# A planner's computed instruction order replaced by a table of another order, in a fused retention and mixture-of-attention kernel

## The chip, the cores and the metric

The program runs on one core of a Trainium2 chip. The metric is the device time of one execution in microseconds (us), lower is better. TensorE is called PE in the rows (PEld are its weight loads), VectorE is DVE, ScalarE is ACT, GpSimd is POOL and SyncE, which issues all transfers here, is SP.

## The reference

Inputs are q, k and v of 4 batches, 8 heads, 768 steps and 64 features. A linear-attention recurrence with a decay per head makes y; its heads side by side are the input x (4 x 768 x 512) of four attention experts, of which each row uses two.

```python
for t in range(S):
    state = gamma[None, :, None, None] * state + np.einsum('bhd,bhe->bhde', k[:, :, t], v[:, :, t])
    y[:, :, t] = scale * np.einsum('bhd,bhde->bhe', q[:, :, t], state)
...
logits = x @ w_gate              # the two largest of 4: softmax weights
for e in range(E):
    q = x @ wq[e]
    k = x @ wk[e]
    v = x @ wv[e]
    scores = scale * (q @ k.transpose(0, 2, 1))
    scores = np.where(causal, -1000000000.0, scores)
    scores = scores - scores.max(-1, keepdims=True)
    a = np.exp(scores)
    a /= a.sum(-1, keepdims=True) + 1e-09
    ye = a @ v @ wo[e]
    ...                          # added to the output of the rows that chose e
```

## The kernel before

The work is cut along time. A *chunk* is 128 steps of a batch for all heads (24 in all). `chunk(g)` is three steps on TensorE: `h1(2g)`, `h2(g, g+1)` and `h1(2g+1)`. An `h1` takes the state's update of a half chunk (L486) and what the state gives to y (L490); `h2` takes the products inside the chunk (L545) and, for the next chunk, q times k (L551). All are 64x64 matmuls in fp32, 128 of them in a chunk as the profile counts them, each with a weight load. DVE evacuates the state into `sblk` (L500) and masks q times k into `am` (L559); GpSimd scales K and Q by decays ahead of it (`kdecay` L425, `qdecay` L440; DVE for chunk 0). ScalarE and DVE split y into a high and a low part, `xh` (L513) and `xl` (L516).

Three chunks are a *group* (8 in all), the unit of the attention. For a group TensorE makes four projections (`proj`, L601, 12 matmuls each) to q and k of a pair of experts; SP moves pieces of them between partitions (L618). Three value/gate products (`vgate`, L643) give v and the gate's logits. Max passes (`mpass`: L724, L737 and L738 on TensorE, L727 and L746 on DVE) find each row's maximum, which `mrow` moves through DRAM into an extra row of q. Then come scores (L850, L851) with the exponential on ScalarE (L857), the sums of its tiles (L872, L879; the first columns copied by ScalarE, L875), products with v (`av`, L896), the normalizer's sums (`norm_a`, L919) and output products (`wout`, L1010, evacuated at L1018).

None of these calls emits an instruction at once. A `Recorder` stores each as an operation with its engine, an assumed cost, the operations it depends on, and the tiles it needs. Tiles come from tags with few slots; all products but the state and `av` share tag `ps`, six PSUM banks. `schedule` then plays the operations through with the assumed costs and latencies, and each time takes the one with the least start time plus 0.01 of its rank; ranks come from the order of recording, of the last operations from the longest path (`by_path`), and are moved at random places by `shift` for 66 seeds. The result is a fixed order for each engine and a slot for each tile, and the program is emitted in it. Each engine works through its own instructions in that order and waits on semaphores where an operand or a slot is not ready. Before all this TensorE runs 12 warm-up matmuls (L1121) on a tile that GpSimd sets to zero, and SP issues the first loads: chunks' tiles `qkT_t` (L410) and `kv_t` (L414), constants (L360), and weight pieces (L379), which ScalarE, DVE and GpSimd split into high and low parts (L385, L386).

Of the kernel before, what the change touches and what calls it, by code (L numbers as in the profile page):

```python
# [3 lines left out]

# [10 lines left out]
AX = mybir.AxisListType  # L15

COL = 0.4545e-3
SWITCH = 0.17
LAT = dict(PE=dict(PE=0.0, DVE=0.2, ACT=0.2, POOL=0.26, SP=0.25),
           DVE=dict(PE=0.16, ACT=0.04, POOL=0.08, SP=0.1),  # L20
           ACT=dict(PE=0.16, DVE=0.04, POOL=0.08, SP=0.1),
           POOL=dict(PE=0.16, ACT=0.06, DVE=0.04, SP=0.1),
           SP=dict(PE=0.16, ACT=0.06, DVE=0.06, POOL=0.1, SP=0.1))
ALPHA = 0.01

COST = dict(chunk=2.2, proj=2.1, vg=1.44, m0=0.35, m1=0.6, g2=0.2, wout=1.4, norm=0.7, mrow=0.1)
MARGIN = 0.0
SWP = 2.0
LEAD_P = 0.0
PATH = 1.0  # L30
LEAD_A = 0.25

SHIFTS = (
# [3 lines left out]
)  # L37


def act_c(n):  # L40
# [11 lines left out]
class Buf:  # L52
    def __init__(self, tag):
        self.tag = tag
        self.slot = None
        self.left = 0
        self.made = None

    @property
# [2 lines left out]


class Tag:
    def __init__(self, tiles, name="", fifo=True):
        self.name = name
        self.fifo = fifo
        self.tiles = tiles
        self.free = [0.0] * len(tiles)
        self.owner = [None] * len(tiles)  # L70
        self.order = []
        self.next = 0


class Op:
    __slots__ = ("eng", "cost", "fn", "mode", "deps", "new", "bufs", "rank", "idx", "start", "end", "users",
                 "waiting", "nbytes", "at")


class Recorder:  # L80
# [6 lines left out]
    def op(self, eng, cost, fn, r=(), w=(), new=(), mode=None, nbytes=0):  # L87
        o = Op()
# [5 lines left out]
        deps = set()  # L94
# [16 lines left out]
            b.tag.order.append(b)  # L111
        o.bufs = {k[0] for k in (*r, *w) if isinstance(k[0], Buf)}
        for b in o.bufs:
            b.left += 1
# [7 lines left out]
    def by_path(self, first, scale):  # L122

        end = max(o.rank for o in self.ops)
        path = {}
        for o in reversed(self.ops):
            tail = path.get(o, 0.0) + o.cost + (1.7 if o.eng == "SP" else 0.0)
            for d in o.deps:
                t = tail + (0.0 if d.eng == o.eng and o.eng != "SP" else LAT[d.eng][o.eng])
                if t > path.get(d, 0.0):  # L130
                    path[d] = t
            if o.idx >= first:
                o.rank = end - scale * tail

    def shift(self, seeds):

        at = [o.rank for o in self.ops]
        span = max(at)
        for seed in seeds:
            rnd = random.Random(seed)  # L140
            w = rnd.choice((20, 40, 80, 400))
            a = rnd.uniform(-w / 2, span - w / 2)
            amp = rnd.choice((0.5, 1.5, 4, 10))
            engines = rnd.choice((("PE",), ("PE", "DVE", "ACT", "POOL", "SP"), ("DVE", "ACT", "POOL", "SP")))
            dens = rnd.choice((0.1, 0.3, 1))
            for o, t in zip(self.ops, at):
                if a <= t < a + w and o.eng in engines and rnd.random() < dens:
                    o.rank += rnd.gauss(0, amp)

    def schedule(self):  # L150
        users = {}
        for o in self.ops:
            o.users = []
        for o in self.ops:
            o.waiting = len(o.deps)
            for d in o.deps:
                d.users.append(o)
        ready = {}
        for o in self.ops:
            ready.setdefault(o.eng, [])  # L160
            if not o.waiting:
                ready[o.eng].append(o)
        T = {e: 0.0 for e in ready}
        mode = None
        bw = 0.0
        out = []
        lastfree = {}

        def est(o):
            t = T[o.eng]  # L170
            for d in o.deps:
                if d.eng == o.eng and o.eng != "SP":
                    e = d.end
                else:
                    e = d.end + LAT[d.eng][o.eng] + (MARGIN if o.eng == "PE" else 0.0)
                if e > t:
                    t = e
            need = {}
            for b in o.new:
                tag = b.tag  # L180
                k = need.get(tag, 0)
                if tag.fifo and tag.order[tag.next + k] is not b:
                    return None
                slots = sorted((tag.free[i], i) for i in range(len(tag.tiles)) if tag.owner[i] is None)
                if len(slots) <= k:
                    return None
                if slots[k][0] + 0.16 + MARGIN > t:
                    t = slots[k][0] + 0.16 + MARGIN
                need[tag] = k + 1
            return t  # L190

        n = len(self.ops)
        while len(out) < n:
            best = None
            for e, lst in ready.items():
                eb = None
                for o in lst:
                    s = est(o)
                    if s is None:
                        continue  # L200
                    sc = max(s, T[e]) + ALPHA * o.rank
                    if e == "PE" and o.mode != mode:
                        sc += SWP * SWITCH
                    if eb is None or sc < eb[0]:
                        eb = (sc, s, o)
                if eb and (best is None or eb[1] < best[1]):
                    best = eb
            assert best is not None, [(o.idx, o.eng) for l in ready.values() for o in l][:20]
            _, s, o = best
            for b in o.new:  # L210
                tag = b.tag
                _, i = min((tag.free[i], i) for i in range(len(tag.tiles)) if tag.owner[i] is None)
                tag.owner[i] = b
                b.slot = i
                tag.next += 1
            o.start = s
            if o.eng == "PE":
                if o.mode != mode:
                    s += SWITCH
                    mode = o.mode  # L220
                o.end = T["PE"] = s + o.cost
            elif o.eng == "SP":
                T["SP"] = s + 0.4
                bw = max(bw, s + 0.4) + o.nbytes / 300e3
                o.end = bw + 1.7
            else:
                o.end = T[o.eng] = s + o.cost
            for b in o.bufs:
                b.left -= 1
                b.tag.free[b.slot] = max(b.tag.free[b.slot], o.end)  # L230
                if not b.left:
                    b.tag.owner[b.slot] = None
            ready[o.eng].remove(o)
            out.append(o)
            for u in o.users:
                u.waiting -= 1
                if not u.waiting:
                    ready[u.eng].append(u)
        self.span = max(o.end for o in out)
        self.busy = {e: sum(o.cost for o in out if o.eng == e) for e in T}  # L240
        self.out = out
        return out

    def replay(self):

        T = {}
        free = {}
        mode = None
        bw = 0.0
        for o in self.out:  # L250
            s = T.get(o.eng, 0.0)
            for d in o.deps:
                s = max(s, d.at if d.eng == o.eng and o.eng != "SP" else d.at + LAT[d.eng][o.eng])
            for b in o.new:
                s = max(s, free.get((b.tag, b.slot), 0.0) + 0.16)
            if o.eng == "PE":
                if o.mode != mode:
                    s += SWITCH
                    mode = o.mode
                o.at = T["PE"] = s + o.cost  # L260
            elif o.eng == "SP":
                T["SP"] = s + 0.4
                bw = max(bw, s + 0.4) + o.nbytes / 300e3
                o.at = bw + 1.7
            else:
                o.at = T[o.eng] = s + o.cost
            for b in o.bufs:
                k = (b.tag, b.slot)
                free[k] = max(free.get(k, 0.0), o.at)
        return max(o.at for o in self.out)  # L270


@with_exitstack
def tile_retention_moe_attention(
# [881 lines left out]
    for s in range(1, NJ):  # L1156
# [3 lines left out]
        merge(ls, (0.0, LEAD_P, LEAD_A))  # L1160
    merge([tail[:]])
    tail[:] = []
    first = len(R.ops)
    merge([stream_p(NJ - 1)])
    merge([stream_a(NJ - 2)])
    merge([stream_a(NJ - 1)])

    if PATH:
        R.by_path(first, PATH)
    R.shift(SHIFTS)  # L1170
    order = R.schedule()
    with tc.manual_schedule():
        for o in order:
            o.fn()


_SHAPES = [((4, 768, 512), "float32")]

# [76 lines left out]
```

## Time and profile before

| | |
|---|---|
| time, median of 3 runs | 330.72 us (329.74 to 331.65) |
| span of the profiled execution, first to last instruction | 326.7 us |
| between that span and the median of the runs | 4.0 us |
| busy: TensorE, its weight loads | 314.3 us (96%), 272.9 us (84%) |
| busy: DVE, ScalarE, GpSimd | 174.7 us (53%), 132.6 us (41%), 170.3 us (52%) |
| chain that ended last, by engine | PE 88%, DMA 7% |
| transfers | 50.82 MB, mean 156 GB/s |

The profile tells of one execution. A busy share is a mean over stages with different limits, so what matters is where the busiest engine stands still, and what ended each such stop. "issue" means that an instruction began late though nothing that the profile shows was waited for. All times are counted from the start of the span.

### The profile page before, as it was taken

To read this page: it belongs to the slowest core of one execution; us is meant where nothing else is said; L and a number is where in the kernel's file an instruction comes from. 1 tells how busy PE (TensorE), PEld (TensorE's weight loads), DVE (VectorE), ACT (ScalarE), POOL (GpSimd) and SP (SyncE) were. 2 spreads that over 40 slices of the span, in tenths; PEclk is the share of its full clock that TensorE was granted. 3 is DMA by queue.
4 is the path that set the end of the run, shared out by engine and by line. 5 is a ranking of instruction groups with operands and counts; after the bars stand their busy time and mean duration, and the time that the engine had idled before them with its cause. 6 is when DMAs were issued, how large, how long until landed. Compare 5 with 4: busy or idle time off the path is not lost.

```text
span 326.7 us, 11233 instructions
## 1 busy us (share of the span) xinstructions
PE 314.3 (96%) x4738; PEld 272.9 (84%) x4738; DVE 174.7 (53%) x478; ACT 132.6 (41%) x322; POOL 170.3 (52%) x189
## 2 busy tenths in 40 slices
PE   7779999999999999999999999999999999999995
PEld 3669989889978799879979788897979789878674
DVE  2574467666443555767242574937452243896733
ACT  1452222533535333524527224432534235428542
POOL 5776251561874976314785854542394361913700
PEclk9999999999999999999999999999999999999999
DMA  7996993355468353535563675352412422413022
GB/s 261 357 403 226 283 324 117 112 142 179 106 188 266 136 181 102 161 124 181 145 160 135 197 237 144 142 164 86 114 45 99 98 49 74 125 69 91 1 99 96
DMA packets 22071, 50.82 MB, mean 156 GB/s; under 512 B 3618, under 2 KB 8310, under 8 KB 22020
## 3 DMA queue, kind: packets, MB, share of 16 engines
q1 hardware_dynamic: 22020, 50.10, 49.0%
q8 instruction: 37, 0.61, 0.8%
q14 instruction: 14, 0.11, 0.1%
HBM read 30.71 MB, written 6.79 MB: 115 GB/s over the span
## 4 chain that ended last, share of the span: by engine, by line
PE 88%; DMA 7%; issue 1%; SPq 1%; DVE 1%; ACT 1%; ACTq 0%
PE ps L601 20%; PE ps L1010 11%; PE ps_o L896 11%; PE ps L643 9%; PE ps L850 7%; PE ps L851 6%; PE ps_st L486 5%; PE ps L551 4%; PE ps L738 4%; DMA kv_t<-in_kv_dram 3%; PE ps L545 2%; DMA qkT_t<-in_qkT_dram 2%; PE ps L490 2%; PE ps L919 2%; PE ps L724 2%; PE ps_st L896 1%
## 5 line engine op out<-in xcount | busy, mean ns | idle before, releaser
L746 DVE CUSTOM_DVE_ANT_0 scr<-ps,cmask_t 128x128 bf16<-128x128 f32 (+3 forms) x64 | 29.7, 487 | 46.6 <-PE ps L738 46.1
L857 ACT ACTIVATE pt<-ps 128x384 f32<-128x384 f32 (+2 forms) x112 | 49.4, 491 | 12.1 <-PE ps L851 9.7
L440 POOL TENSOR_TENSOR qd<-qkT_t,qdec_t 128x512 f32<-128x512 f32 (+1 forms) x23 | 28.3, 1232 | 41.4 <-PE ps L490 26.2
L601 PE MATMUL ps<-xh,qk_hi 128*128 128x384 f32 x128 | 44.1, 345 | 0.0
L850 PE MATMUL ps<-q,k 128*128 128x384 f32 (+2 forms) x144 | 43.4, 316 | 0.0
L601 PE MATMUL ps<-xh,qk_lo 128*128 128x384 f32 x128 | 43.1, 337 | 0.0
L601 PE MATMUL ps<-xl,qk_hi 128*128 128x384 f32 x128 | 43.1, 336 | 0.0
L851 PE MATMUL ps<-q,k 65*128 65x384 f32 (+2 forms) x144 | 42.1, 312 | 0.0
L879 POOL TENSOR_TENSOR ac<-ac,pt 128x256 f32<-128x256 f32 (+2 forms) x32 | 39.9, 1247 | 3.1 <-ACT pt L857 1.2
L863 POOL TENSOR_SCALAR_AFFINE_SELECT pt<-pt 128x256 f32<-128x256 f32 x48 | 20.1, 426 | 38.9 <-ACT pt L857 38.2
L896 PE MATMUL ps_o<-pt,vt 128*64 128x384 f32 (+2 forms) x252 | 36.2, 422 | 0.0
L606 ACT ACTIVATE k<-ps 128x384 fp32r<-128x384 f32 x32 | 15.7, 491 | 50.0 <-PE ps L601 50.0
L425 POOL TENSOR_TENSOR kv_t<-kv_t,kdec_t 128x512 f32<-128x512 f32 (+1 forms) x23 | 22.2, 968 | 23.0 <-DMA kv_t<-in_kv_dram 23.0
L486 PE MATMUL ps_st<-kv_t 64*64 64x64 f32 x704 | 30.2, 222 | 1.7 <-POOL kv_t L425 0.7
L490 PE MATMUL ps<-qd,sblk 64*64 64x64 f32 x704 | 29.8, 221 | 0.8 <-issue 0.8
L872 POOL TENSOR_TENSOR ac<-pt,pt 128x512 f32<-128x512 f32 (+1 forms) x14 | 21.3, 1523 | 17.5 <-ACT pt L857 17.1
L486 PEld LDWEIGHTS ps_st<-kv_t 64*64 64x64 f32 x704 | 24.9, 134 | 6.2 <-issue 4.0
L896 PEld LDWEIGHTS ps_o<-pt,vt 128*64 128x64 f32 x252 | 16.4, 136 | 16.0 <-issue 11.9
L513 ACT ACTIVATE xh<-ps 128x512 fp32r<-128x512 f32 x24 | 14.3, 598 | 37.4 <-PE ps L490 35.6
L643 PE MATMUL ps<-vg_hi,xh 128*128 128x260 f32 x96 | 28.0, 291 | 1.5 <-ACT xh L513 1.5
L850 PEld LDWEIGHTS ps<-q,k 128*128 128x128 f32 x144 | 27.3, 190 | 2.4 <-issue 2.0
L500 DVE TENSOR_TENSOR sblk<-ps_st,sdec_t 128x256 f32<-128x256 f32 x44 | 18.5, 420 | 19.8 <-PE ps_st L486 18.4
(115 smaller groups left out, 777.6 us busy)
## 6 DMA issues: line engine op xcount, KB each, us to landing
qkT_t<-in_qkT_dram SPq DMA_DIRECT2D x24, 512.0 KB
kv_t<-in_kv_dram SPq DMA_DIRECT2D x24, 512.0 KB
out_dram<-ot SPq DMA_DIRECT2D x24, 256.0 KB
q<-k SPq DMA_DIRECT2D x28, 192.0 KB
k<-k SPq DMA_DIRECT2D x14, 192.0 KB
k<-q SPq DMA_DIRECT2D x14, 192.0 KB
fe<-fd SPq DMA_DIRECT2D x28, 96.0 KB
pt<-in_wqk_dram SPq DMA_DIRECT2D x4, 256.0 KB
```

The lines of the kernel that those rows point to most:

```text
L440: e.tensor_tensor(halves(qd.t), halves(qb.t[:, 0]), K["qdec"][:, :, None, :].to_broadcast([128, HP, n, SC]), op=OP.mult)
L486: nc.tensor.matmul(ST[b].t[rows(rt), s * D:(s + 1) * D], kvs(m, 0, s)[rows(rt)], kvs(m, 1, s)[rows(rt)], start=c == 0 and s == 0, stop=Fal ...
L490: nc.tensor.matmul(yo(m, rt, s), SB[m % 2][rows(rt), s], LD[g, 2].t[rows(rt), s, m % 2 * SC:(m % 2 + 1) * SC], start=m % 2 == 0 and s == 0 ...
L601: nc.tensor.matmul(pb.t[:, :HS], ww[:, kt, wsl], xx[:, kt], start=n == 0, stop=n == 11)
L643: nc.tensor.matmul(pb.t[:, :NV + E], xx[:, kt, sl], ww[:, kt], start=n == 0, stop=n == 11)
L746: lambda: nc.vector.tensor_tensor_reduce(scr.t[:, :n1], pb.t[:, :n1], K["cmask"][:, HS + C - n1:], 1.0, mx0.t[:, e, i:i + 1] if prior else ...
L850: nc.tensor.matmul(o, k1.t[:, e, ko:ko + C], q1.t[:, e, q0:], start=True, stop=False)
L851: nc.tensor.matmul(o, k2.t[:65, e, ko:ko + C], q2.t[:65, e, q0:], start=False, stop=True)
L857: lambda es=es, sb=sb, n=n: nc.scalar.activation(pt.t[:, es[0]:es[0] + n, q0:], sb.t[:, :n * w].rearrange("p (e t) -> p e t", e=n), AF.Exp ...
L879: op(eng, cost, lambda: en.tensor_tensor(ac.t[:, :, q0:], ac.t[:, :, q0:], pt.t[:, :, q0:], op=OP.add), r=[(pt, 0), (pt, 1), (ac, "b")], w ...
L896: nc.tensor.matmul(ob.t[e * 64:e * 64 + 64, q0:HS], vt.t[:, ko // C, ee * 64:ee * 64 + 64], pt.t[:, e, q0:], start=kb == 0, stop=kb == las ...
L1010: nc.tensor.matmul(wb.t, oo[:, sl], ww[:, p], start=n == 0 and p == 0, stop=n == 2 and p == NP - 1)
```

## The change

The operations, their dependencies and what each emits stay as they are. `schedule`, `by_path`, `shift` and `replay` go, with their constants. In their place stand two tables: `ORDER`, 1,555 numbers of operations in the order in which they are emitted, and `SLOTS`, which gives the slot of each new tile by tag. `arrange` looks both up. The table is not what the planner computed: on TensorE 213 of 510 operations keep their place in the engine's order, and on SP 59 of 224.

```diff
-    def schedule(self):
...
+    def arrange(self, order, slots):
+
+        turns = {name: iter(row) for name, row in slots.items()}
+        out = [self.ops[i] for i in order]
+        for o in out:
             for b in o.new:
...
+                b.slot = int(next(turns[b.tag.name]))
         return out
...
-    if PATH:
-        R.by_path(first, PATH)
-    R.shift(SHIFTS)
-    order = R.schedule()
     with tc.manual_schedule():
-        for o in order:
+        for o in R.arrange(ORDER, SLOTS):
             o.fn()
+
+ORDER = (
+    3, 1, 2, 5, 6, 4, 7, 12, 8, 13, 9, 10, 14, 19, 20, 21, 99, 0, 23, 100, 101, 102, 103, 26, 1313, 24, 25, 22, 28,
...
+SLOTS = {
+    "ac": "010101010101010101",
```

The first place is SP's queue, from its eighth issue on; the seven before it are the same transfers with the first K/V tile put first. In the names, `ot`, `ac` and `pt` are tiles that hold weight pieces at the start (value/gate, then q/k). Before:

```order
L410 DMA qkT_t_64<-in_qkT_dram 128x1024
L379 DMA ot_127<-in_wvg_dram 128x260
L379 DMA ot_128<-in_wvg_dram 128x260
L379 DMA ac_116<-in_wvg_dram 128x260
L379 DMA ac_117<-in_wvg_dram 128x260
L414 DMA kv_t_67<-in_kv_dram 128x1024
L410 DMA qkT_t_65<-in_qkT_dram 128x1024
L414 DMA kv_t_68<-in_kv_dram 128x1024
L379 DMA pt_110<-in_wqk_dram 128x512
```

And now:

```order
L245 DMA qkT_t_64<-in_qkT_dram 128x1024
L249 DMA kv_t_67<-in_kv_dram 128x1024
L214 DMA ot_127<-in_wvg_dram 128x260
L245 DMA qkT_t_65<-in_qkT_dram 128x1024
L214 DMA ot_128<-in_wvg_dram 128x260
L214 DMA ac_116<-in_wvg_dram 128x260
L249 DMA kv_t_68<-in_kv_dram 128x1024
L245 DMA qkT_t_63<-in_qkT_dram 128x1024
L214 DMA ac_117<-in_wvg_dram 128x260
L214 DMA pt_110<-in_wqk_dram 128x512
```

The K/V tile of chunk 1 and the q/k tiles of chunks 2 and 3 (`qkT_t_65`, and `qkT_t_63` for the second time) now stand among the value/gate pieces or ahead of them; line numbers are lower by 165 in the changed kernel. On TensorE the first value/gate product moves from before chunk 1 to behind chunk 2's first half, and the second to behind chunk 2.

The second place is TensorE at the border of chunks 17 and 18, the end of a batch (near 186 us before). The first row below ends chunk 17's products; then come chunk 17's last half, chunk 18's first half and its `h2`. Before:

```order
L545 MATMUL ps_141<-am_72,kv_t_68 64x64
L490 MATMUL ps_141<-qd_70,sblk_156 64x64 x8
L486 MATMUL ps_st_147<-kv_t_66 64x64 x8
L551 MATMUL ps_144<-qkT_t_64 64x64
L545 MATMUL ps_145<-am_71,kv_t_66 64x64
```

And now:

```order
L325 MATMUL ps_143<-qd_70,sblk_156 64x64 x8
L321 MATMUL ps_st_147<-kv_t_66 64x64 x8
L845 MATMUL ps_144<-wo_hi,oh_121 128x512
L845 MATMUL ps_144<-wo_lo,oh_121 128x512
L845 MATMUL ps_144<-wo_hi,ol_123 128x512
L845 MATMUL ps_144<-wo_hi,oh_122 128x512
L845 MATMUL ps_144<-wo_lo,oh_122 128x512
L845 MATMUL ps_144<-wo_hi,ol_124 128x512
L573 MATMUL ps_141<-k_4_87,q_0_77 128x256
L754 MATMUL ps_145<-ac_116,sel 32x128 x2
L754 MATMUL ps_145<-ac_117,sel 32x128 x2
```

Between chunk 18's first half and its `h2` there now stand an output product, a max pass and the normalizer's 12 sums (24 matmuls in the profile; the first rows of them are shown).

The third place is TensorE at the last projections of group 5 (near 203 us before), where a max pass reads keys of a projection before. The first rows end a projection. Before:

```order
L601 MATMUL ps_144<-xh_74,qk_hi 128x384
L601 MATMUL ps_144<-xl_76,qk_hi 128x384
L601 MATMUL ps_144<-xh_74,qk_lo 128x384
L737 MATMUL ps_145<-k_1_84,q_1_78 128x384
L738 MATMUL ps_145<-k_2_85,q_1_78 128x128
L737 MATMUL ps_140<-k_1_84,q_1_78 128x384
L738 MATMUL ps_140<-k_2_85,q_1_78 128x128
```

And now:

```order
L436 MATMUL ps_145<-xh_74,qk_lo 128x384
L436 MATMUL ps_141<-xh_74,qk_hi 128x384
L436 MATMUL ps_141<-xl_76,qk_hi 128x384
L436 MATMUL ps_141<-xh_74,qk_lo 128x384
...
L436 MATMUL ps_141<-xh_74,qk_lo 128x384
L572 MATMUL ps_142<-k_3_86,q_1_78 128x384
L573 MATMUL ps_142<-k_2_85,q_1_78 128x128
```

The group's fourth projection (into `ps_141`) now stands between the third and the first max pass, which is followed by a value/gate product.

## Rows read from the trace of the kernel before

**Rows 1.** The page: busy time, share, instructions; and an instruction queue.
```profile
PE 314.3 (96%) x4738; PEld 272.9 (84%) x4738; DVE 174.7 (53%) x478; ACT 132.6 (41%) x322; POOL 170.3 (52%) x189
...
q8 instruction: 37, 0.61, 0.8%
```

**Rows 2.** Windows: length, busy us by engine (instructions), granted clock, DMA share, GB/s.
```profile
0.00:25.00 25.00, 18.72 (x451) 14.10 (x452) 12.92 (x28) 9.21 (x21) 17.29 (x26) 1.00 0.95 341
25.00:100.00 75.00, 74.25 (x1281) 67.87 (x1284) 41.06 (x119) 26.16 (x66) 36.74 (x39) 1.00 0.62 187
```

**Rows 3.** Timeline of TensorE: start, length, what, and the idle time before it.
```profile
20.21 0.27 PE L545 MATMUL ps<-am,kv_t 64*64 64x64 f32 x1 [0.95 <-issue]
45.50 0.21 PE L490 MATMUL ps<-qd,sblk 64*64 64x64 f32 x1 [0.75 <-issue]
188.57 0.27 PE L486 MATMUL ps_st<-kv_t 64*64 64x64 f32 x1 [0.47 <-issue]
203.86 0.33 PE L738 MATMUL ps<-k,q 128*128 128x128 f32 x1 [0.76 <-DMA k<-q]
225.86 0.30 PE L919 MATMUL ps<-ac,sel 128*32 128x128 f32 x2 [0.38 <-issue]
```

**Rows 4.** Waits of the weight loads after 25 us: total, times, longest.
```profile
PEld ps_o L896 <- issue: 11.9, 63, 0.4
PEld ps_st L486 <- issue: 4.0, 15, 0.6
PEld ps L490 <- issue: 0.9, 1, 0.9
```

**Rows 5.** Windows, from one stall's end to the next one's.
```profile
20.21:45.50 25.29, 23.58 (x636) 22.11 (x637) 13.88 (x29) 6.96 (x17) 11.71 (x12) 1.00 0.87 286
45.50:188.56 143.06, 142.60 (x2291) 127.16 (x2290) 76.08 (x217) 58.72 (x142) 84.99 (x89) 1.00 0.53 161
188.56:225.85 37.29, 36.15 (x510) 32.45 (x511) 22.78 (x58) 14.26 (x37) 17.06 (x20) 1.00 0.49 149
```

**Rows 6.** Windows: two code blocks of 64x64 work, and one chunk.
```profile
42.04:45.50 3.46, 2.71 (x142) 2.44 (x135) 2.40 (x5) 0.60 (x1) 1.73 (x2) 1.00 0.89 260
107.33:110.43 3.10, 3.10 (x130) 2.32 (x128) 0.79 (x2) 0.05 (x1) 3.02 (x4) 1.00 0.00 0
28.74:30.76 2.02, 2.02 (x129) 1.95 (x128) 1.24 (x3) 0.49 (x1) 0.00 (x0) 1.00 0.13 33
```

**Rows 7.** Timeline of TensorE in the first 25 us.
```profile
10.97 0.39 PE L643 MATMUL ps<-vg_hi,xh 128*128 128x260 f32 x1 [0.74 <-ACT xh L513]
16.19 0.24 PE L486 MATMUL ps_st<-kv_t 64*64 64x64 f32 x1 [0.67 <-POOL kv_t L425]
24.36 0.28 PE L643 MATMUL ps<-vg_hi,xl 128*128 128x260 f32 x1
24.48 0.34 PE L601 MATMUL ps<-xh,qk_hi 128*128 128x384 f32 x1
24.65 0.34 PE L601 MATMUL ps<-xl,qk_hi 128*128 128x384 f32 x1
```

**Rows 8.** Timeline of DVE: a weight split.
```profile
9.41 0.85 DVE L386 TENSOR_TENSOR vg_lo<-ot,vg_hi 128x260 fp32r<-128x260 f32 x1 [0.68 <-ACT vg_hi L385]
```

**Rows 9.** Waits of TensorE in the first 25 us: total, times, longest.
```profile
PE ps L643 <- ACT xh L513: 1.5, 2, 0.7
PE ps L551 <- DMA qkT_t<-in_qkT_dram: 0.7, 2, 0.4
PE ps_st L486 <- DVE kv_t L425: 0.5, 1, 0.5
```

**Rows 10.** Lines: a max pass on DVE; count, busy us, mean ns, idle before.
```profile
L727 DVE TENSOR_REDUCE mx<-ps 128x1 f32<-128x384 f32 x32 | 16.9, 552 | 8.2 <-PE ps L724 8.0
```

**Rows 11.** Timeline of ScalarE: the copy before which an output product was evacuated.
```profile
134.53 0.41 ACT L875 ACTIVATE ac<-pt 128x256 f32<-128x256 f32 x1
```

More of the change, by code (lines that the diff above doesn't have):

```diff
@@ L17 @@
 COL = 0.4545e-3
[L18 to L24, printed above, removed]
 COST = dict(chunk=2.2, proj=2.1, vg=1.44, m0=0.35, m1=0.6, g2=0.2, wout=1.4, norm=0.7, mrow=0.1)
-MARGIN = 0.0
-SWP = 2.0
 LEAD_P = 0.0
-PATH = 1.0
 LEAD_A = 0.25
-SHIFTS = (
[3 rows of a table removed]
-)
 def act_c(n):
@@ L55, in __init__ @@
         self.slot = None
-        self.left = 0
         self.made = None
@@ L64, with __init__ @@
 class Tag:
-    def __init__(self, tiles, name="", fifo=True):
+    def __init__(self, tiles, name, fifo=True):
         self.name = name
@@ L68, in __init__ @@
         self.tiles = tiles
-        self.free = [0.0] * len(tiles)
-        self.owner = [None] * len(tiles)
         self.order = []
-        self.next = 0
 class Op:
-    __slots__ = ("eng", "cost", "fn", "mode", "deps", "new", "bufs", "rank", "idx", "start", "end", "users",
-                 "waiting", "nbytes", "at")
+    __slots__ = ("eng", "cost", "fn", "mode", "deps", "new", "bufs", "rank", "idx", "nbytes")
 class Recorder:
@@ L113, in op @@
         for b in o.bufs:
-            b.left += 1
             if b in o.new:
@@ L120, in op @@
         return o
[L122 to L148, printed above, removed]
@@ L150, in schedule @@
-    def schedule(self):
[L151 to L178, printed above, removed]
-            for b in o.new:
[L180 to L241, printed above, removed]
-        return out
@@ L244, in replay @@
[L244 to L270, printed above, removed]
+    def arrange(self, order, slots):
+        turns = {name: iter(row) for name, row in slots.items()}
+        out = [self.ops[i] for i in order]
+        for o in out:
+            for b in o.new:
+                b.slot = int(next(turns[b.tag.name]))
+        return out
@@ L1162, in tile_retention_moe_attention @@
     tail[:] = []
-    first = len(R.ops)
+    R.first = len(R.ops)
     merge([stream_p(NJ - 1)])
@@ L1166, in tile_retention_moe_attention @@
     merge([stream_a(NJ - 1)])
-    if PATH:
-        R.by_path(first, PATH)
-    R.shift(SHIFTS)
-    order = R.schedule()
     with tc.manual_schedule():
-        for o in order:
+        for o in R.arrange(ORDER, SLOTS):
             o.fn()
+ORDER = (
[74 rows of a table added]
+)
+SLOTS = {
+    "ac": "010101010101010101",
+    "am": "010101010101010101010101",
+    "f": "0000000",
+    "fd": "0101010",
+    "fe": "0000000",
+    "ge": "0000",
+    "gg": "0000",
+    "gs": "0000",
+    "k1": "0123402134201324",
+    "k2": "0123402134201324",
+    "kv_t": "012012012012012012012012",
+    "lg": "0101",
+    "md": "01010101010101",
+    "mt": "01010101010101",
+    "mx": "0101010101010101",
+    "mx0": "01010101",
+    "mz": "00",
+    "oh": "0101010101010101",
+    "ol": "0101010101010101",
+    "on": "0120120120120120",
+    "ot": "01210210102102102102102102",
+    "ps": (
+        "0123450123450214352104315204135024150315251340512340152401523150423510431502413052341035412035410235"
+        "4120530241503245132405324102540314034013520143051234051350423502315024531204135021432045301254021543"
+        "0251243025413024530125032513041520301254310243512043125043210451320415203452104320135401253142503142"
+        "5312403512105421305421305241254352041530421350421350214351203451205312035410324510324124530125402531"
+        "405231405231502"
+    ),
+    "ps_o": "00000000000000",
+    "ps_st": "000000",
+    "pt": "012345021354021354021354021354021354021354021354021354021350214350503214503214",
+    "q1": "0120120120120120",
+    "q2": "0120120120120120",
+    "qd": "010101010101010101010101",
+    "qkT_t": "012012012012012012012012",
+    "rw": "010101",
+    "scr": "011010011010101010101010100110101001101000101010100110101010101010101010101001011001101001010010",
+    "vt": "01201201",
+    "wn": "0101",
+    "wt": "0101",
+    "xh": "01010101",
+    "xl": "01010101",
+}
 _SHAPES = [((4, 768, 512), "float32")]
```

1 line of the change is left out of this document (removed), and 76 rows, old and new, of tables (ORDER, SHIFTS).

## The prediction

> **What bounds the kernel now.** I read the page first. TensorE is busy 96% of the span and no other engine more than 53% [rows 1]. So an order of instructions can only win back time in which TensorE stands still, or lose more. Next the span by stretches: of the first 25 us TensorE works 18.72, of the following 75 it works 74.25, at a granted clock of 1.00, the upper level of 2.4 GHz, in both [rows 2]. So two things are open to an order: the first 25 us with 6.3 us idle, and the few stalls behind them.
>
> In the timeline after 25 us four stalls of TensorE are longer than 0.3 us. One, of 0.76 at 203.86, ends with a DMA; three, of 0.75, 0.47 and 0.38, end on "issue", on nothing that the profile shows [rows 3]. They lie in the middle of runs of small matmuls whose operands do not change there. A fourth of that kind, of 0.95, is at 20.21 [rows 3]. The weight loads, which run ahead of the matmuls, stand somewhat longer: 0.9 for the first, 0.6 for the second [rows 4].
>
> What do the "issue" stalls share? Between one and the next TensorE ran 636+637, 2291+2290 and 510+511 matmuls and loads [rows 5]: 1273, 4581 and 1021, which is 5, 18 and 4 times about 255. The page has 4738+4738 of them and 37 transfers on the instruction queue q8 [rows 1], so 256 instructions to a transfer. The stalls stand at borders of blocks of code, and I take them for waits for the next block. Whether a border stalls would then depend on how fast the block before it is used up: the block from 42.04 on, nothing but 64x64 matmuls, took 3.46 us with its stall, so 2.7 by TensorE's own work, and one of 3.10 passed without any [rows 6].
>
> The Trainium skill ("Runtime: NRT & Kernel Launch", section "Instruction fetch mechanics") also has code come in blocks of 256 instructions, but calls the cost of a crossing "mostly hidden". The trace agrees on the size; of 37 crossings it shows four that are not hidden. By that sentence alone the second term below would be nought.
>
> **The change part by part.** The same instructions run; their places and tile slots are others. The sum is made against the profiled execution: its span is 326.7, and the runs' median of 330.72 has 4.0 us around it, left as they are.
>
> *The first 25 us.* Before, SP issues all four value/gate weight pieces ahead of the second K/V tile, shown in the first excerpt above. TensorE does the first value/gate product at 10.97 after a wait of 0.74, reaches chunk 2's first half at 16.19 after 0.67 more for GpSimd's decay of K, and the first projection at 24.48 [rows 7]. Now chunks 1 and 2 come first, and their tiles are loaded first. Chunk 2's first half hardly moves all the same: the state goes through DVE, where the new order puts two weight splits (0.85 was one [rows 8]) and an xl ahead of the evacuation of chunk 1's state, while the pieces to split land later. I take 16.0. Behind it stand three value/gate products instead of two, but one of them now covers the wait for xh and xl of chunk 2 (up to 0.7), and the wait for a q/k tile (up to 0.4) goes, since that tile is loaded earlier [rows 9]. The work from there on is a chunk, 2.0 us as from 28.74 to 30.76 [rows 6], and three products of 12 matmuls at 0.12 from start to start [rows 7], 1.45 each: 6.4. The block stall of 0.95 stays, as the border falls into the same chunk: 7.3. The projection starts at about 23.3 to 23.5: **-1.0 us**. Bounds: -2.2 (no block stall either) and +0.5 (DVE holds chunk 1 up for longer).
>
> *Three block stalls.* In the first dense block the new order sets two max passes between the chunks, and a max pass and a whole projection ahead of the second chunk's last half; in the second an output product, a max pass and the normalizer's sums (the second excerpt above); in the third the sums are followed by an output product and max passes in place of chunk work before them. Each adds over 1.5 us to blocks of 2.4 to 2.7, which takes them past the 3.10 that passed [rows 6]. No other block behind the first 25 us becomes noticeably denser than it was where it passed. So -(0.75+0.47+0.38) = -1.6 by the matmuls [rows 3], and -1.9 with the loads' 0.9 and 0.6 for the first two [rows 4]: I take **-1.9**; nought if other borders stall instead.
>
> *The DMA wait at 203.86* (0.76 [rows 3]) is for a copy of keys between partitions. The new order puts a second projection ahead of the max pass that waits (third excerpt): 12 matmuls of 0.17 from start to start [rows 7], 2.0 us, which covers it. **-0.8**, or nought if the copy is issued later by as much.
>
> *New waits.* (a) At about 60 to 64 us the last projection of its group is moved behind a row of max passes, so six of these follow each other with four score products between. DVE needs about 0.55 for each [rows 10], TensorE 0.2 to 0.4, and six PSUM banks lie between them. Price 0 to 1.6; I take 0.5. (b) At about 135 us ScalarE's evacuation of an output product went ahead of an exponential and a copy (0.41 [rows 11]); now it stands behind both, and its bank is held longer by the copy and about as much for the exponential. Price 0 to 0.8; I take 0.3. (c) Max passes or scores nearer to what they need at about 204, 271 and 279 us: 0 to 1.6; I take 0.3. Together **+1.1** (0 to 4.0).
>
> *Tile shapes.* TensorE changes between 64x64, 64-column, 32-column and full tiles 81 times instead of 75. The nearest row is what the loads of the av products wait for "issue", 11.9 us in 63 cases [rows 4], so 0.19 for one, or 0 where hidden. Six more are 0 to 1.1; I take **+0.4**.
>
> Costed at nothing: the memset that the warm-up matmuls wait for comes two memsets later, but the first chunk waits 0.5 us for DVE's decay of K anyhow [rows 9]. Without that cover it is 0.7. The end of the program is the same output product in both.
>
> Sum: -1.0 - 1.9 - 0.8 + 1.1 + 0.4 = -2.2: a span of 324.5, and 330.7 - 2.2 = **328.5 us**.
>
> **The rivals.**
> 1. *The stalls go and nothing comes for them.* The first 25 us give 2.0, the stalls 2.7, six shapes cost 0.2: 330.7 - 4.5 = 326.2. For it: no engine that TensorE waits for is over 53% busy [rows 1]. Against it: the bunches of (a) and (b) can be read in the order.
> 2. *The "issue" stalls stay.* If a border stalls for what the instruction queue does just then and not for density, three of them are left or others stall: -1.0 - 0.8 + 1.1 + 0.4 = -0.3, so 330.4. For it: 3.10 passed, hardly more than the blocks that stalled, and dense ones are left. Against it: all four fell into the densest stretches. (The skill's sentence, with crossings hidden, would give this time too.)
> 3. *Slower: the banks fill.* The place is the bunches of (a) to (c). If DVE and ScalarE fall behind by more than six banks hold, TensorE waits as long as they lag: the prices at their upper ends are 4.0, shapes 1.1, the first 25 us 0, so 5.1 - 1.9 - 0.8 = +2.4: 333.1. It decides once the new waits and shapes together pass 4 us. For it: DVE's 0.55 against TensorE's 0.2 for a max pass. Against it: from 25 to 100 us DVE works only 41 of 75 us [rows 2].
>
> That the change doesn't do what it says is excluded: the excerpts show other orders on SP and TensorE.
>
> **How the numbers follow.** Forecast 0.52, rival 1 0.18, rival 2 0.18, rival 3 0.12. A measurement of this kernel can tell about 0.5%, 1.65 us, from no change. The forecast lies 2.2 below with about 1.3 to either side, so two thirds to three quarters of its 0.52 are faster and the rest the same; with all of rival 1 and a little of rival 2 that makes 0.60 faster, 0.29 same and 0.11 slower. The likeliest case alone has 327.2 to 329.8. The range takes in rivals 1 and 2 and ends half way to rival 3: 325.6 to 331.8.
>
> **What would show it.** In the changed kernel the first projection starts before 24 us; after 25 us no "issue" stall of 0.4 us or more is left in the 64x64 runs; the DMA wait near 200 us is gone; and the longest new waits are those of max passes or score products near 60 us. I am wrong if "issue" stalls of the old length stand at other borders of 256, if the projection starts at 24.5 or later, or if TensorE's waits after 25 us pass 4 us in all.

## The result and the profile after

The changed kernel takes 327.93 us (median of 12 runs, 326.41 to 329.93), the kernel before, on the same chip, 330.92 us (12 runs, 329.02 to 332.65). The ratio is 0.9915, with a 95% interval of 0.9886 to 0.9944: faster, by 3.0 us or 0.9%, a small change but clear of the noise. The forecast was 328.5. Times here and below are medians of all runs, while ratios and intervals are of the fast runs alone, those within 1.5% of the quickest of their kernel. The total came out nearly as forecast; several of its terms did not.

The page of the changed kernel, as in [rows 1]:

```profile
PE 315.4 (97%) x4738; PEld 274.7 (84%) x4738; DVE 172.3 (53%) x478; ACT 130.1 (40%) x322; POOL 169.7 (52%) x189
...
q8 instruction: 37, 0.61, 0.7%
```

The same instructions run, and TensorE is as busy. Next the windows as in [rows 2], with two stretches of the first 25 us by themselves (length, busy us of each engine, granted clock, DMA share, GB/s):

```profile
0.00:25.00 25.00, 18.50 (x436) 14.41 (x437) 11.18 (x26) 6.67 (x12) 15.70 (x24) 0.86 0.95 347
25.00:100.00 75.00, 74.58 (x1272) 68.19 (x1270) 42.68 (x124) 27.36 (x71) 38.10 (x40) 1.00 0.60 175
15.00:20.00 5.00, 3.94 (x87) 3.52 (x79) 4.17 (x8) 3.16 (x6) 2.47 (x3) 0.63 1.01 373
20.00:25.00 5.00, 5.00 (x113) 4.70 (x113) 1.15 (x3) 0.60 (x1) 2.79 (x2) 0.69 1.04 387
```

The start did not get better. TensorE works 0.2 us less in it than before, and from 15 to 25 us the granted clock is 0.63 and 0.69: for part of the time it stood at the lower of its two levels, 1.2 GHz. The waits of TensorE in the first 25 us say what came first (as in [rows 9]; total, times, longest):

```profile
PE ps L380 <- issue: 2.3, 1, 2.3
PE ps L956 <- POOL wu L917: 2.3, 1, 2.3
PE ps_st L321 <- POOL kv_t L260: 0.7, 1, 0.7
PE ps_st L321 <- issue: 0.6, 1, 0.6
PE ps_st L321 <- DVE sblk L335: 0.5, 1, 0.5
PE ps L380 <- DVE am L394: 0.2, 1, 0.2
```

The waits for xh (1.5) and for a q/k tile (0.7) are gone. In their place stands one "issue" stall of 2.3 us in a chunk's second half (line 380, which was line 545 before: all lines of the kernel stand 165 lower now). The timeline has it at 14.54, and the first projection (line 436) at 26.45, where [rows 7] had 24.48:

```profile
14.54 0.21 PE L380 MATMUL ps<-am,kv_t 64*64 64x64 f32 x1 [2.26 <-issue]
...
15.74 0.27 PE L321 MATMUL ps_st<-kv_t 64*64 64x64 f32 x1 [0.51 <-DVE sblk L335]
...
17.04 0.34 PE L321 MATMUL ps_st<-kv_t 64*64 64x64 f32 x1 [0.56 <-issue]
...
26.45 0.34 PE L436 MATMUL ps<-xh,qk_hi 128*128 128x384 f32 x1
```

Behind the first 25 us nearly all waits of TensorE are gone; the waits view of 25 to 330 us has this one row, where [rows 3] had four stalls:

```profile
PE ps L436 <- issue: 0.4, 1, 0.4
```

It is at 49.38, in the projection that the new order put into the first dense block. The max pass whose second matmul waited at 203.86 for the copy of keys (line 738, now 573) now runs at 206.14 and 206.33 without a wait, right behind the projection set ahead of it:

```profile
205.96 0.34 PE L436 MATMUL ps<-xh,qk_lo 128*128 128x384 f32 x1
206.14 0.35 PE L572 MATMUL ps<-k,q 128*128 128x384 f32 x1
206.33 0.22 PE L573 MATMUL ps<-k,q 128*128 128x128 f32 x1
```

From the first projection to TensorE's last matmul the changed kernel took 295.9 us, and the profiled execution of before 298.7. So against that execution the start lost 2.0 us and the rest won 2.8.

### The profile page after: what moved, and what is told of

Read it like the earlier page. It is cut to its first block, busy times and chain, and to the rows that moved or that the text cites. A ratio compares the mean times of both kernels' runs of the same rounds, so it can differ in the third digit from the quotient of the medians.

```text
span 325.9 us, 11205 instructions
## 1 busy us (share of the span) xinstructions
PE 315.4 (97%) x4738; PEld 274.7 (84%) x4738; DVE 172.3 (53%) x478; ACT 130.1 (40%) x322; POOL 169.7 (52%) x189
## 3 DMA queue, kind: packets, MB, share of 16 engines
HBM read 30.71 MB, written 6.79 MB: 115 GB/s over the span
## 4 chain that ended last, share of the span: by engine, by line
PE 94%; DMA 3%; DVE 1%; issue 1%; ACT 1%; SPq 0%; ACTq 0%; DVEq 0%
PE ps L436 21%; PE ps L478 11%; PE ps L845 11%; PE ps_o L731 10%; PE ps L685 7%; PE ps L686 7%; PE ps_st L321 6%; PE ps L386 5%; PE ps L573 4%; PE ps L559 2%; PE ps L325 2%; PE ps L380 2%; PE ps L754 2%; DMA ot<-in_wvg_dram 2%; PE ps_st L731 1%; DMA am_t<-in_amask_dram 1%
## 5 line engine op out<-in xcount | busy, mean ns | idle before, releaser
L698 POOL TENSOR_SCALAR_AFFINE_SELECT pt<-pt 128x256 f32<-128x256 f32 x48 | 20.9, 445 | 50.1 <-ACT pt L692 39.8
L685 PE MATMUL ps<-q,k 128*128 128x384 f32 (+2 forms) x144 | 43.9, 318 | 0.0
L686 PE MATMUL ps<-q,k 65*128 65x384 f32 (+2 forms) x144 | 42.2, 313 | 0.0
L731 PE MATMUL ps_o<-pt,vt 128*64 128x384 f32 (+2 forms) x252 | 35.5, 421 | 0.0
L380 PE MATMUL ps<-am,kv_t 64*64 64x64 f32 x768 | 27.8, 223 | 2.5 <-issue 2.3
L478 PE MATMUL ps<-vg_hi,xh 128*128 128x260 f32 x96 | 28.8, 300 | 0.0
```

Of the source, the lines that this page charges most:

```text
L380: nc.tensor.matmul(yo(2 * g + u, rt, s), kvs(u + 2 * g, 1, s)[rows(rt)], amg.t[rows(rt), u, s], start=g % NC == 0 and u == 0 and s == 0, s ...
L478: nc.tensor.matmul(pb.t[:, :NV + E], xx[:, kt, sl], ww[:, kt], start=n == 0, stop=n == 11)
L685: nc.tensor.matmul(o, k1.t[:, e, ko:ko + C], q1.t[:, e, q0:], start=True, stop=False)
L686: nc.tensor.matmul(o, k2.t[:65, e, ko:ko + C], q2.t[:65, e, q0:], start=False, stop=True)
L731: nc.tensor.matmul(ob.t[e * 64:e * 64 + 64, q0:HS], vt.t[:, ko // C, ee * 64:ee * 64 + 64], pt.t[:, e, q0:], start=kb == 0, stop=kb == las ...
```

## The experiments

Theory (T): the gain is in the order behind the start, by the borders of code blocks. Rivals: the new start makes the gain; the places of the tiles make it; fewer waits make it, whatever the borders. Each set of runs had the kernel before beside it, with medians of 331.27 us (e1 to e4), 332.77 (e5 to e8) and 330.93 (e9 to e12); ratios are to it.

### The kernel before, once more, and with its borders moved

The first (e3_before_again) is the kernel before, without an edit:

> The kernel before, unchanged, to see a second profile and the clock of each run. Theory: the same three issue stalls at the same instructions, the DMA wait, first projection at 24.5 us and no fall of the clock in most runs. Rival: other runs of it lose time in the first 25 us too, as the changed kernel does, and the profile shown was a lucky one (a span of 327.5 or more).

It took 331.05 us (10 runs). This execution, close to its median, loses more in the same places than the one shown first:

```profile
21.87 0.27 PE L545 MATMUL ps<-am,kv_t 64*64 64x64 f32 x1 [1.85 <-issue]
...
26.13 0.34 PE L601 MATMUL ps<-xh,qk_hi 128*128 128x384 f32 x1
...
47.71 0.21 PE L490 MATMUL ps<-qd,sblk 64*64 64x64 f32 x1 [1.30 <-issue]
```

The stalls of 0.95 and 0.75 [rows 3] are 1.85 and 1.30 here, the first projection starts at 26.13, not 24.48, and the rest takes 299.8 us. Its span is 329.5 and its time 331.22: 1.7 us lie around a span, in this and in every other execution profiled whose time is known, but for e6 (2.1). So the execution of [rows 1 to 11], with a span of 326.7, was one of some 328.4 us, quicker than the kernel mostly is.

The second (e4_border_shift) is the kernel before with 64 more instructions of TensorE ahead of all work, a load and a narrow matmul 32 times:

```diff
+            for i in range(32):
+                nc.tensor.matmul(pbs[i % 6].t[:, :64], wu, wu[:, :64], start=True, stop=True)
```

> The kernel before with 32 more small warm-up matmuls (64 instructions with their loads) ahead of all work, while TensorE would wait anyhow. Theory (stalls at borders of 256 instructions): every border falls 64 instructions earlier in the program, so the stalls move to other instructions: from the last half of chunk 6 into its h2 step (L545, L551), from the first half-steps of chunk 18 into its h2, a new one of about 0.7 us in the last half of chunk 12 near 112 us, and none in the sums of group 4 near 225 us. Rival (the stalls belong to what these instructions need): they stay at L490 of chunk 6, L486 of chunk 18 and L919 of group 4, and none comes at chunk 12.

One run: 338.78 us. The stalls moved to other instructions, and to the border again, which the rival excluded. They are more and longer than I had listed, and behind the one that ends at 158.32 the granted clock fell as well (0.62 from 158.3 to 162.5). In the timeline:

```profile
19.89 0.36 PE L490 MATMUL ps<-qd,sblk 64*64 64x64 f32 x1 [2.96 <-issue]
...
50.68 0.21 PE L545 MATMUL ps<-am,kv_t 64*64 64x64 f32 x1 [1.73 <-issue]
```

With all loads, matmuls and waits of TensorE numbered in the order of their starts, every one of these stalls falls at 193 + 256 n. The table holds the gaps of over 0.25 us between the starts of the two instructions at a border (number: start, gap, us), worked out from the traces:

```
before            705: 20.21 1.17  1985: 45.50 0.97   6593: 188.57 0.68  7617: 225.86 0.66
e3_before_again   449: 15.02 0.58  705: 21.87 2.07    1985: 47.71 1.52   6593: 192.25 1.27
e4_border_shift   705: 19.89 3.18  1985: 50.68 1.95   3777: 109.96 1.62  4289: 120.34 1.14
                  5313: 158.32 1.92  6593: 199.85 0.65
changed           449: 14.54 2.48  1985: 49.38 0.76   4033: 111.31 0.31  4289: 116.18 0.27
e5_after_again    449: 14.54 2.45  1729: 44.99 1.26   4033: 112.73 0.31  4289: 118.42 1.09
```

So the "issue" stalls at these numbers are waits for code: shown. (One in e3 is not: at 164.93, at no border, TensorE's queue waits for the landing of a copy of keys, issued at 161.31, whose last part comes at 164.84. The view calls it "issue" too.) An instruction behind a stalled border, at gaps of over 0.5 us, starts 1.2 to 1.6 us after the landing of its block's 16-KB transfer on the instruction queue (47.71 after 46.35 in e3, 49.38 after 47.91 and 14.54 after 13.14 in the changed kernel). In the first 25 us, at a DMA share of about 1.0, a block's transfer also starts late: in before 3.66 us after the border ahead of it, against 1.23 for the one that ended the stall at 45.50.

### The start and the rest apart

e1_old_start has the planner's first instructions on each engine (14 of TensorE, 22 of DVE, 20 of ScalarE, 21 of GpSimd, 30 DMAs) and the table's order behind them; e2_new_start has it the other way round. In both a tile takes the place that has been free longest. The first row of the order in the changed kernel and in e1:

```diff
-    3, 1, 2, 5, 6, 4, 7, 12, 8, 13, 9, 10, 14, 19, 20, 21, 99, 0, 23, 100, 101, 102, 103, 26, 1313, 24, 25, 22, 28,
+    22, 2, 19, 20, 0, 1, 21, 23, 3, 99, 4, 5, 100, 6, 7, 101, 8, 102, 9, 10, 103, 11, 12, 1313,
```

> The first operations of every engine, up to the first projection (14 on TensorE, 22 on VectorE, 20 on ScalarE, 21 on GpSimd, 30 on SyncE), in the order of the kernel before, everything behind them in the order of the changed kernel. Theory (the first 25 us of the new order cost about 2 us, what stands behind them gives about 3): first projection at about 24.5 us, clock 2.4 GHz all through, and 1 to 2 us faster than the changed kernel, 326 to 327 us. Rival (the first 25 us are worth nothing either way, since their loss lay in one execution): the changed kernel's time, 328 us. Rival 2 (the new first loads are where the gain comes from): 330 us or more.

> The opposite half: first operations in the new order, everything behind them in the order of the kernel before. Theory: first projection at 26 us with a wait of 2 us on issue in chunk 1 and a fall of the clock to 1.2 GHz behind it; the block stalls near 45, 188 and 225 us and the DMA wait near 204 us are all there; 332 to 333 us, slower than before. Rival: 331 us, as before. Rival 2: 328 us, as the changed kernel.

e1: 331.39 us, ratio 1.004 (1.0009 to 1.0072). e2: 332.45 us, ratio 1.0038 (1.0005 to 1.0071). Neither half had the gain, which none of the theories had expected of both. But both had also dealt out the tiles' places anew. So that was tried by itself, beside the changed kernel unchanged (e5_after_again):

> The changed kernel once more, unchanged, to see how much of its time is chance. If its gain is the order's, 327.9 us within 0.5, ratio to before about 0.991, first projection near 26.4 us and about 295.9 us from there to TensorE's last end. If the profile of the changed kernel was a lucky execution, as the one of the kernel before was, the rest is 297 to 298 us instead.

e5: 328.25 us, ratio 0.9867 (0.9811 to 0.9923). The profiled execution was its slowest, 331.24, and shows what chance does: stalls of 1.0 at another border (44.99) and 0.8 at 118.42, and 1.4 for the copy of keys, 0.9 of it at 283.34:

```profile
PE ps L573 <- DMA k<-q: 1.4, 2, 0.9
PE ps L380 <- issue: 1.0, 1, 1.0
PE ps L754 <- issue: 0.8, 1, 0.8
```

e6_slots_lru keeps the changed kernel's order on every engine and deals out only the PSUM banks (348 of 415 change) and eight places of the ring pt anew:

```diff
     "ps": (
-        "0123450123450214352104315204135024150315251340512340152401523150423510431502413052341035412035410235"
+        "0123450123450214315204321504230512405340104235041352405124503452103541234051243501323450123451203451"
```

> The changed kernel's order on every engine, word for word, but of the table that names the tiles' places only the PSUM banks (and eight places of one ring) are dealt out anew, to the place that has been free longest: 348 of the banks differ. If the order alone makes the gain, 327.9 us as the changed kernel. If the choice of banks makes a part of it (which the two half-and-half kernels had also lost), 329.5 to 331.5 us, with small losses spread over scores, maxima and weighted sums.

e6: 331.40 us, ratio 0.9984 (0.9949 to 1.0019). The same order with other banks has no gain. Its waits of TensorE after 25 us:

```profile
PE ps_o L731 <- issue: 0.6, 1, 0.6
PE ps L572 <- ACT ot L853: 0.5, 1, 0.5
PE ps L685 <- ACT pt L692: 0.2, 1, 0.2
```

Two of these are waits for ScalarE to empty a bank. "Free longest" was decided by the order in which instructions are written down, and there the bank of the output product at 292 us came up just as ScalarE had begun to empty it. Most of the loss is in smaller pieces: compared operation by operation with e7 (below), whose order is the same from there on, score products take 1.4 us more (0.9 on L685 and 0.6 on L686), max passes 0.7 (the wait at 292 us), output products 0.5, and weighted sums 1.2, of which 0.9 is a border at 112.27 that e7 passes. Another 0.4 of the 3.2 us between e6 and e5 lies around the span.

e7_old_start_kept and e8_new_start_kept are the two halves again, now with the table's own places behind the start (only 6 banks of the start differ from the changed kernel, as the first row of e7's banks shows) and, in e8, with the planner's own places:

```diff
     "ps": (
-        "0123450123450214352104315204135024150315251340512340152401523150423510431502413052341035412035410235"
+        "0123450120345124352104315204135024150315251340512340152401523150423510431502413052341035412035410235"
```

> The planner's first instructions (14 of TensorE's, 22 of VectorE's, 20 of ScalarE's, 21 of GpSimd's, 30 DMAs) and behind them the table's order with the table's own places for every tile. If the order behind the start and the choice of places carry the gain, the first projection at 25.4 us as in the earlier half-and-half kernel and 296 us behind it: about 327 us. If the new start is what makes the rest quick (its fetches of instruction blocks and its clock), 331.4 us again.

> The table's first instructions, and behind them the planner's order with the planner's own places for every tile. If the rest carries the gain, no faster than before: first projection at 26.2 us and 299 to 300 us behind it, 330.5 to 331.5 us. If the new start carries it, 328 us.

e7: 328.00 us, ratio 0.9862 (0.9815 to 0.9910), as the changed kernel in the same set. e8: 335.74 us, ratio 1.0093 (1.0056 to 1.0131). So the rest of the table, with its places, carries the whole gain, and the new start adds nothing to it: shown. Set ahead of the planner's rest, the new start costs 3 us and not the nothing I had expected. There TensorE waits 2.1 us for the value tile that ScalarE evacuates, 2.1 at a border and 1.8 for the copy of keys:

```profile
PE ps L478 <- ACT vt L494: 2.1, 1, 2.1
PE ps L325 <- issue: 2.1, 1, 2.1
PE ps L573 <- DMA k<-q: 1.8, 1, 1.8
PE ps_st L321 <- issue: 1.1, 1, 1.1
PE ps L754 <- issue: 0.6, 1, 0.6
```

e2, with the same order and other places, lost less (ratio 1.0038). Its trace (an execution of 335.42 us, that of e8 took 336.70) lacks the first of these waits, and its first projection starts at 26.19, in e8 at 28.16; behind it the two take about as long (304.0 and 303.3 us). So the planner's places behind another start cost this wait, as far as one trace of each can tell.

### The borders moved under both orders

If the rest's gain is where its borders fall, it must go when the borders move, and the two orders must then be level. In e9_table_shift96 and e10_planner_shift96 TensorE has 96 instructions more ahead of all work. The warm-up was meant to last as long as before, but the first matmul of the work starts 1.1 to 1.7 us later for it, at 8.54 in e9 (6.79 in the changed kernel) and at 7.49 in e10 (5.83 and 6.42 in the two traces of the kernel before):

```diff
-            for i in range(12):
+            for i in range(9):
                 nc.tensor.matmul(pbs[i % 6].t, wu, wu[:, None, :].to_broadcast([128, 4, 128]), start=True, stop=True)
+            for i in range(51):
+                nc.tensor.matmul(pbs[i % 6].t[:, :64], wu, wu[:, :64], start=True, stop=True)
```

> The changed kernel, with three of the twelve warm-up matmuls replaced by 51 narrow ones: 96 more instructions on TensorE ahead of the first projection, and not one behind it. Counted on the changed kernel's trace, the borders of its blocks of 256 instructions then close eight blocks that take under 3.1 us each (1.9 to 3.1), where now three do, together 9.1 us short of 3.7 us a block, where now 2.4. If the gain over the kernel before is mostly where the borders fall, it is gone: 331 to 335 us, with issue stalls near 56, 99, 146, 165 and 218 us. If it is the order's own (fewer waits, whatever the borders), 327.5 to 329 us still, 3 us under the planner's order with the same shift.

> The kernel before with the same 96 instructions. Its blocks are then 9.2 us short of 3.7 us each, where they are 5.5 short unshifted, and so as badly cut as the changed kernel's with this shift. If the borders make the difference between the two kernels, 333 to 335 us, within 1 us of the changed kernel with the shift. If the order makes it without the borders, 331 to 332 us or, should the borders cost both alike, 3 us over the shifted table.

e9: 339.86 us, ratio 1.0271 (1.0180 to 1.0363). e10: 340.73 us, ratio 1.0261 (1.0190 to 1.0332). Both are far slower than I expected. Between their medians 0.9 of the 3 us are left, but with four runs each, from 338.65 to 342.96 and from 338.92 to 341.86, a difference of 3 us would hardly stand out. From the first projection on, the profiled executions (the quickest of e9, the slowest of e10) take 306.1 us with the table's order and 305.2 with the planner's.

That does not make the borders the cause, since they did not hit both alike, as I had counted on. Worked out as in the table above, the gaps behind the first projection are 9.0 us in e9 and 6.3 in e10. Without them 297.1 and 298.9 are left, so the table's order is still 1.8 us ahead, with a fall of the clock in both. Unshifted it is 2.5 ahead by the same working (294.5 in the changed kernel, 297.1 in e3). The test shows that borders can cost more than the whole gain, and not that they are the gain.

Waits of TensorE after 25 us, of e9:

```profile
PE ps L386 <- issue: 4.2, 2, 3.1
PE ps L754 <- issue: 2.1, 1, 2.1
PE ps L685 <- issue: 1.5, 1, 1.5
PE ps L478 <- issue: 1.1, 1, 1.1
```

All 8.9 us are borders (at 961, 1985, 2497, 5313 and 6593). The Trainium skill ("Runtime: NRT & Kernel Launch", section "Instruction fetch mechanics") calls crossings "mostly hidden"; here eight of 37 show, with gaps of 13.6 us, counting those in the first 25 us. A long one costs more than its gap. After the stall of 3.15 at 50.35 in e9 the granted clock was 0.50, all of the time the lower level, and then 0.92 (windows):

```profile
50.40:55.00 4.60, 4.60 (x47) 4.48 (x47) 1.74 (x5) 0.00 (x0) 2.09 (x2) 0.50 0.87 275
55.00:60.00 5.00, 5.00 (x59) 4.59 (x58) 2.60 (x10) 1.61 (x4) 1.30 (x1) 0.92 0.33 111
```

At half the clock TensorE does the work of 2.3 us in these 4.6, so this border cost some 5.5 us in all, an estimate from these rows. The same in e10 after a stall of 2.45 at 20.97:

```profile
20.00:25.00 5.00, 4.03 (x42) 3.69 (x46) 1.66 (x2) 0.24 (x1) 3.07 (x3) 0.55 1.02 363
25.00:30.00 5.00, 3.64 (x99) 3.16 (x100) 2.08 (x4) 2.28 (x6) 0.40 (x1) 0.77 0.39 124
30.00:35.00 5.00, 5.00 (x24) 5.00 (x24) 1.44 (x1) 0.53 (x3) 4.58 (x4) 0.66 0.48 190
```

Its first projection starts at 31.37. That is why the times passed my 331 to 335: I had added up gaps, and left out the clock and the start. In e9 the gaps came out in their sum (9.0 us behind the first projection, where I had 9.1), but not at my places.

The last two move the borders the other way, by 12 instructions, behind the table's and the planner's start:

```diff
-            for i in range(12):
+            for i in range(6):
```

> The changed kernel with six warm-up matmuls less: 12 instructions fewer ahead of the first projection. On its trace only 0.6 us are then short of 3.7 us a block, where now 2.4. If the borders carry stalls as the theory says, the stall near 49 us goes and 0.7 to 1.5 us with it: 326.5 to 327.3 us, unless the shorter warm-up costs the first microseconds their clock. If the borders are of no account, 327.9 us or a little more.

> The planner's first instructions with the table's order and places behind them (328.0 us with twelve warm-up matmuls), and six warm-up matmuls less. By its trace 0.2 us are then short of 3.7 us a block, where now 1.8. The borders' theory expects 326.3 to 327.3 us, and with it a kernel a little faster than the changed one; without it, 328 us.

e11: 327.31 us (4 runs, 327.12 to 328.11), ratio 0.9867 (0.9806 to 0.9927). e12: 328.32 us, ratio 0.9897 (0.9823 to 0.9971). e11 is the quickest median here, though not by more than its interval, and e12 missed the 326.3 to 327.3 that I had given it. The stall of e11 near 49 us has not gone, though I had expected that; it is shorter:

```profile
49.53 0.27 PE L321 MATMUL ps_st<-kv_t 64*64 64x64 f32 x1 [0.32 <-issue]
```

My count was of blocks that take under 3.7 us, which lies between the 3.46 and 4.01 us that the stalled block ahead of number 1985 took in before and in e3. The block before this border takes 5.7 in the changed kernel; it stalls because its transfer starts 2.76 us after the border ahead, at a DMA share of 1.07. So short blocks are not the only ones that stall: a late fetch does it too, and the count forecasts only the bad shifts. No version beat the changed kernel clearly.

## Why the prediction was right, and where it was not

*The sum* put the kernel at -2.2 us; it is -3.0 between the medians. Against the execution that it was made from, the span went from 326.7 to 325.9, so by -0.8, and the forecast had 324.5. That the time came out is partly luck: a base that was off made up for a start that got slower. By two of its own signs the working was wrong, a projection that starts at 24.5 or later (26.45) and an "issue" stall at another border (2.26, at 449). The steps:

*The base.* "The runs' median of 330.72 has 4.0 us around it, left as they are" was wrong: 1.7 lie around a span, and the other 2.3 were a typical execution's longer stalls, as e3 shows. The change could save some of these, and the sum had no term for it.

*The first 25 us* (-1.0, bounds -2.2 to +0.5): the step failed. It cost 2.0 us against the execution shown, 0.3 against e3. The waits named as covered, for xh and for the q/k tile, did go [rows 9]. Two things came in their place. "I take 16.0" for chunk 2's first half became 17.04: DVE's two weight splits and the xl, which I had named, stand ahead of the evacuation of the state, and the splits took 0.78 and 1.26 where I had 0.85 for one [rows 8]:

```profile
12.79 0.78 DVE L221 TENSOR_TENSOR vg_lo<-ac,vg_hi 128x260 fp32r<-128x260 f32 x1 [1.84 <-ACT vg_hi L220]
13.49 1.26 DVE L221 TENSOR_TENSOR vg_lo<-ot,vg_hi 128x260 fp32r<-128x260 f32 x1
14.67 0.68 DVE L351 SCALAR_TENSOR_TENSOR xl<-ps,xh 128x512 fp32r<-128x512 f32 x1
15.27 0.41 DVE L335 TENSOR_TENSOR sblk<-ps_st,sdec_t 128x256 f32<-128x256 f32 x1
```

And "the block stall of 0.95 stays, as the border falls into the same chunk" did not hold: the border at 705 passes (a gap of 0.08 us at 21.58). The one at 449, passed in 0.12 us before, now stalls 2.26 with the transfer landing at 13.14, and the clock falls behind it (0.63 and 0.69 until 25 us, 1.00 before [rows 2]). The clock is the larger part: from 17.04 to the projection are 9.4 us, where the working had 6.4 of work, and the two windows have lost some 3.4 us to it (0.37 and 0.31 of 5 us each, an estimate), most of them behind 17.04. e7 has the planner's start, its first projection 0.7 us earlier (25.77), and the same time as the changed kernel.

*Three block stalls* (-1.9): the mechanism was right, and e4, e9 and e10 show it. The stalls at 188.57 and 225.86 are gone, the one at 45.50 is smaller and stands on the projection moved there. By the gaps at borders after 25 us, 2.31 before (2.79 in e3) and 1.34 after, the term was worth -1.0 to -1.45 in these executions, so it was sized too large; in e5, an execution 3 us over its median, other borders took it back (2.66). "Density" was only half of it, as e11 shows.

*The DMA wait at 203.86* (-0.8): gone from that place in every trace of the table's order, as the working has it.

*New waits* (+1.1): mis-sized, they are nought in the changed kernel's first trace, where no row of the waits after 25 us is a max pass, a score product or an output product. Of (c) one came in other traces: the max pass near 279 us waits for a copy of keys, 0.92 us at 283.34 in e5 and 0.73 at 281.93 in e7. The six banks, as the table deals them out, held for (a) and (b). How near waits for banks are, e6 shows: the same order with other banks takes 3.2 us more, a border's 0.9 among them.

*Tile shapes* (+0.4): not settled. Behind the first projection the shape changes 69 times before and 77 times after. Steps over a change take 0.15 to 0.42 us from start to start, in all 15.0 us before and 16.4 after. What the same steps would take without a change is not known, so the term lies between nought and 1.4.

*The rivals.* Nothing new came, as in rival 1, yet its gain in the first 25 us was lost. Rival 2 ("other borders stall") is what the shift of 96 makes of the change. What stays open is how much of the 3.0 us is borders. Of the 4.0 us from the first projection on, between the changed kernel's trace and e3 (both near their medians), 1.45 are. Waits for copies of keys are 1.3 (at 164.93 and 207.26 in e3), some 0.4 lie in two gaps at the gate's last weights and the output product behind them (L704 and L1010, near 291 us in e3), and 0.8 I could not place. Waits for copies come and go from execution to execution (1.4 us in e5, none in the first trace of the same kernel), so how much of this is the order's own stays open too.

## What to carry to other kernels

Number the instructions of the busiest engine and look where the borders of code blocks fall, before an order is called better: 96 instructions put ahead of it made the reordered kernel 12 us slower, four times what the reordering had won. When half an order is tried, keep the other half's places for tiles as well; banks dealt out by the written order alone cost as much as the reordering had won. And add terms up against an execution that lies at the median, not against whichever was profiled.

## What the runs showed of the hardware

A stall at a code border can cost twice. Behind stalls of 2.26, 2.45 and 3.15 us the granted clock was 0.63, 0.55 and 0.50 (windows of some 5 us above), while behind 1.85 in e3 it stayed at 1.00:

```profile
20.00:25.00 5.00, 2.19 (x90) 1.83 (x90) 1.97 (x5) 1.95 (x4) 2.73 (x3) 1.00 1.04 404
```

The length of the stall alone does not decide it. In e10 the clock fell behind a shorter one, of 1.67, and in e8 it did not behind a longer one, of 2.10 (the first two rows are of e10, the last three of e8):

```profile
54.20 0.21 PE L545 MATMUL ps<-am,kv_t 64*64 64x64 f32 x1 [1.67 <-issue]
54.20:59.00 4.80, 4.80 (x78) 4.68 (x78) 2.67 (x7) 0.60 (x1) 2.63 (x3) 0.64 0.91 306
...
51.61 0.21 PE L325 MATMUL ps<-qd,sblk 64*64 64x64 f32 x1 [2.10 <-issue]
48.00:53.00 5.00, 2.90 (x103) 2.56 (x100) 2.27 (x5) 0.97 (x2) 2.92 (x3) 1.00 0.97 316
53.00:58.00 5.00, 5.00 (x35) 4.96 (x34) 3.15 (x14) 1.13 (x3) 2.62 (x3) 1.00 0.48 162
```

And instructions that compute nothing are no neutral edit: with 96 more of them in the warm-up the changed kernel takes 339.9 us. With 12 fewer it takes 327.3, no clear change from 327.9.
